# Attention with decay and a routed layer in one kernel: slot ids and gates in a table of their own, stores of x one step later, five last tiles through one-hot products

## The chip, the cores and the metric

The kernel runs on one core of a Trainium2 chip. The metric is the time of one execution on the device, in microseconds (us); the median of three runs is compared.

## The reference

There are 4 batches, 8 heads, 768 positions and a head dimension of 48, all in float32. First comes an attention whose state decays per channel, then a layer that sends each row to one of 8 experts:

```
for t in range(S):
    state = alpha[:, :, t, :, None] * state + einsum('bhd,bhe->bhde', k[:, :, t], v[:, :, t])
    y[:, :, t] = einsum('bhd,bhde->bhe', q[:, :, t], state)
x = y.transpose(0, 2, 1, 3).reshape(3072, 384)
out = x.copy()
do_compute = x @ w_skip > 0
logits = x[do_compute] @ w_gate                 # 8 experts
e_idx, gate_w = argmax(logits), softmax(logits)[argmax]
out[row] = x[row] + gate_w * (relu(x[row] @ w1[e]) @ w2[e])   # rows with do_compute, e = e_idx[row]
```

Each expert has w1 of 384 x 1024 and w2 of 1024 x 384.

## The kernel before, in words

The rows of x are cut into 24 tiles of 128 positions. The attention loop of `static_path` has a step i for each tile; four batches take turns, so that tile i belongs to batch i % 4. It is a software pipeline: in step i the loads of tile i+4 are issued, the decay products of tile i+3 are made (`decay`: on VectorE the scans `pfx`, L250, and `sfx`, L258, then on POOL two products into `qka`, L261 and L262), the scores of tile i+1 (`scores`, `causal`), the output of tile i (`inter`, `outer`, `carry`, `intra`), and the rows of tile i-1 (`rows`): TensorE turns the output into rows of x and gate logits (`ps_g`), VectorE reduces the logits (L355) and ScalarE copies x out (L360). All instructions stand in the order of the code; each engine runs its own in that order, and so do the queues that issue DMAs (SyncE's, called SP, and POOL's).

SP's queue carries the loads of `qka` (two DMAs a tile, into one of 5 buffers, L237) and of `vt` (L240, 5 buffers), a store of each tile's x to `out` (L362), pieces of expert weights (`raw`, L515), and once the clearing of the slot table (`clear`, L152).

Routing finds for each row its expert and its place in that expert's list. The list is the table `xs` in DRAM: 3072 slots for each expert, two words each, a row's id and its gate. `scatter` (L497, on POOL) writes one tile's 128 pairs to their slots with an indirect DMA. The id is made by an iota on POOL (L359) into column 384 of the tile of x, the gate is copied or written into column 385, and the scatter reads these two columns. The first 256 slots of each expert are worked on; `empty` marks unused ones.

The first expert starts before the last tiles are in its list. The rows of tiles 0 to LATE-1 that belong to expert 0 are fetched by their ids: `early_rows` reads expert 0's slots (`meta0`, L450, which waits for the scatters so far) and `fetch_rows` gathers the rows from `out` (L457, two gathers on POOL). The tiles from LATE on, three before the change, enter by a product: `late_split` splits x into a high and a low half (ScalarE L479, POOL L480), `route_slot` makes a one-hot row `hot` of each row's slot (L443), and `late_rows` multiplies (L466). Gathered and multiplied rows meet in the same PSUM tiles `x0t` (`early_turn`, L472, adds the gathered ones); the zero rows which `clear_late` writes to `out` in the place of late tiles keep the gather harmless. The remaining scatters follow at the end of the loop. In the expert stage `metas` (L555) reads all slots, `gather` fetches the rows of the next experts, `up` and `down` (L607, L623) are the two matmuls in three products of high and low halves, and `split_pieces` (L531, L535) splits the next expert's weights. `guard` reads alpha again (L571) and tests its range on ScalarE (L575).

Of the kernel before, what the change touches and what calls it, by code (L numbers as in the profile page):

```python
# [42 lines left out]
RW = 2 * D + E + 1  # L43
XW = DM + 2
BIG = 32768.0
# [4 lines left out]
WARM0, WARMB = 12, 2  # L50
LATE = NT - 3
DECAY_MIN = 1e-18
# [3 lines left out]
class Kernel:  # L56
# [40 lines left out]
    def constants(self):  # L97
# [36 lines left out]
        self.slot = const.tile([P, NT, 1], U32, name="slot")  # L134
        self.gate = const.tile([P, NT], F32, name="gate")

# [46 lines left out]
    def attention_pools(self, st):  # L183
        tc, nc = self.tc, self.nc
        self.vp = st.enter_context(tc.tile_pool(name="vp", bufs=5))
        self.sc = st.enter_context(tc.tile_pool(name="sc", bufs=2))
        self.xp = st.enter_context(tc.tile_pool(name="xp", bufs=9))
        self.sm = st.enter_context(tc.tile_pool(name="sm", bufs=2))
# [157 lines left out]
    def rows(self, i):  # L346

        nc, w = self.nc, self.work[i]
        if i < NT - 1:
            pg = self.ps_g.tile([P, NP, RW], F32, name="ps_g")  # L350
        else:
            pg = self.ps_v.tile([P, NP, RW], F32, name="ps_v")
        for p in range(NP):
            nc.tensor.matmul(pg[:, p, :], lhsT=w["xt"][:PD, p, :], rhs=self.xw[:PD, p, :], start=True, stop=True)  # L354
        nc.vector.tensor_reduce(out=self.logit[:, i, :], in_=pg[:, :, 2 * D:].rearrange("p a e -> p e a"),  # L355
                                op=ALU.add, axis=AX.X)
        x = self.xp.tile([P, XW], F32, name="x")
        row = self.row(i)
        nc.gpsimd.iota(x[:, DM:DM + 1].bitcast(I32), pattern=[[0, 1]], base=row, channel_multiplier=1)  # L359
        nc.scalar.copy(out=x[:, 0:DM].rearrange("p (a w) -> p a w", a=NP), in_=pg[:, :, 0:2 * D])  # L360
        w["x"] = x
        nc.sync.dma_start(out=self.out[row:row + P, :], in_=x[:, 0:DM])  # L362

# [30 lines left out]
    def route_one(self, i):  # L394
# [16 lines left out]
        yield nc.vector.tensor_scalar(out=s1, in0=s1, scalar1=1e-9, scalar2=None, op0=ALU.add)  # L411
        yield nc.vector.reciprocal(self.work[i]["x"][:, DM + 1:DM + 2], s1)

# [32 lines left out]
    def early_rows(self):  # L446
# [5 lines left out]
        self.early = [ins.ins.name]  # L452
        self.fetch_rows(self.xr0, meta)

# [20 lines left out]
    def late_split(self, i):  # L475

        nc, w = self.nc, self.work[i]
        hi, lo = w["parts"] = [self.late.tile([P, DM], F32R, name=f"late{n}{i}") for n in "hl"]
        nc.scalar.copy(out=hi, in_=w["x"][:, 0:DM])  # L479
        nc.gpsimd.tensor_tensor(lo, w["x"][:, 0:DM], hi.bitcast(F32), ALU.subtract)  # L480

# [10 lines left out]
    def scatter(self, i):  # L492
        nc = self.nc
        x = self.work[i]["x"]
        if i < SOLO:
            nc.gpsimd.tensor_copy(x[:, DM + 1:DM + 2], self.gate[:, i:i + 1])  # L496
        ins = nc.gpsimd.indirect_dma_start(  # L497
            out=self.xs[:, :], out_offset=bass.IndirectOffsetOnAxis(ap=self.slot[:, i, :], axis=0),
            in_=x[:, DM:DM + 2], in_offset=None, bounds_check=E * N - 1, oob_is_err=False)
        self.disjoint(ins.ins, "xs")  # L500
        if i >= LATE:
            for name in self.early:
                self.follow(ins.ins, name)
# [274 lines left out]
    def static_path(self, ctx):  # L778
# [8 lines left out]
        ends = {g[1] - 1: g for g in groups}  # L787
        pending, split, fetch = [], iter(()), iter(())

# [4 lines left out]
        with ExitStack() as st:  # L794
# [14 lines left out]
            for i in range(NT):  # L809
                if i + 4 < NT:  # L810
                    self.load(i + 4)
                if i == 2:
                    self.clear()
# [38 lines left out]
                self.outer(i)  # L852
                self.carry(i)
                if i == NT - 1:
                    assert not pending
                    self.early_rows()
                    self.intra(i)
                    self.route_rank(ends[i - 2])
                    self.small = self.route_slot(ends[i - 2])
                    self.tick(99)  # L860
                    ranked = ends[i - 2]
                if i == NT - 1:
                    self.rows(i - 1)
                if i < NT - 1:
                    self.intra(i)
                if ranked and SOLO - 1 <= i - 2 < LATE:
                    pending += range(*ranked)
                for _ in range(1 if i < SOLO else 2):
# [5 lines left out]
                if i - 1 in ends:  # L874
                    g = ends[i - 1]
                    self.small = chain(self.small, self.route_one(i - 1) if i - 1 >= SOLO else self.route_expert(g))
                    if i - 1 >= SOLO - 1:
                        self.tick(4 if i == NT - 1 else 99)
                    if i - 1 == LATE:
                        self.late_split(LATE)  # L880
            a, b = NT - 2, NT - 1
            self.late_split(a)
            self.rows(b)
            self.late_split(b)
            ps = self.ps_s.tile([P, 2, NP * P], F32, name="ps_s")
            self.x0t = [ps[:, 0, :CAP], ps[:, 1, :CAP], self.ps_g.tile([P, CAP], F32, name="ps_g")]
            self.route_rank((a, b))
            for k in range(KT):
                self.late_rows(LATE, k)
            self.early_turn(0)  # L890
# [12 lines left out]
            self.first_turn()  # L903
            for i in range(LATE, NT):
                self.scatter(i)
# [77 lines left out]
```

## Time and profile before

| what | before |
|---|---|
| median of three runs | 342.89 us (342.66 to 347.0) |
| the profiled execution | 343.51 us, of which 341.8 us are the span of its instructions |
| granted clock of TensorE, mean | 0.897 |
| busy: TensorE, VectorE, ScalarE, POOL | 298.9, 230.1, 153.3, 201.3 us |
| attention steps | to about 170 us |
| first matmul of the experts | 183.83 us |
| HBM read, written | 52.87 MB, 8.50 MB |

A row of the timeline has the start in us from the span's first instruction, the duration, the engine, the line of the kernel, the operation, the tiles (output <- inputs), and in brackets how long the engine was idle before it and what released it. SPq rows are DMAs being issued; they land later. PEld is the weight load of TensorE.

### The profile page before, as it was taken

To read this page: it belongs to the slowest core of one execution; us is meant where nothing else is said; L and a number is where in the kernel's file an instruction comes from. 1 tells how busy PE (TensorE), PEld (TensorE's weight loads), DVE (VectorE), ACT (ScalarE), POOL (GpSimd) and SP (SyncE) were. 2 spreads that over 40 slices of the span, in tenths; PEclk is the share of its full clock that TensorE was granted. 3 is DMA by queue.
4 is the path that set the end of the run, shared out by engine and by line. 5 is a ranking of instruction groups with operands and counts; after the bars stand their busy time and mean duration, and the time that the engine had idled before them with its cause. 6 is when DMAs were issued, how large, how long until landed. Compare 5 with 4: busy or idle time off the path is not lost. (4 is left out here: it accounts for less than half of the span.)

```text
span 341.8 us, 7389 instructions
## 1 busy us (share of the span) xinstructions
PE 298.9 (87%) x2778; PEld 276.1 (81%) x2778; DVE 230.1 (67%) x457; ACT 153.3 (45%) x300; POOL 201.3 (59%) x222
## 2 busy tenths in 40 slices
PE   6869869997997799889839699999989899999991
PEld 5758758886876688668729599999979899999990
DVE  8997495999999999998435623819265456555310
ACT  6114232533344344222531635959496885555200
POOL 6184254697787879757334575756647476764311
PEclk9658967996999969757978989999999999999998
DMA  8949898898669868942815174959769495741000
GB/s 231 294 90 146 186 213 221 207 189 200 177 140 188 207 130 173 191 135 74 125 40 146 37 232 153 381 172 318 263 223 338 148 360 202 244 160 66 16 22 23
DMA packets 27692, 60.33 MB, mean 177 GB/s; under 512 B 6944, under 2 KB 13646, under 8 KB 27648
## 3 DMA queue, kind: packets, MB, share of 16 engines
q1 hardware_dynamic: 24704, 54.67, 60.3%
q0 software_dynamic: 2944, 5.11, 4.4%
q8 instruction: 24, 0.39, 0.5%
q14 instruction: 20, 0.16, 0.2%
HBM read 52.87 MB, written 8.50 MB: 180 GB/s over the span
## 5 line engine op out<-in xcount | busy, mean ns | idle before, releaser
L261 POOL TENSOR_TENSOR qka<-qka,sfx 112x512 f32<-112x512 f32 x22 | 26.8, 1218 | 44.5 <-DVE sfx L258 30.0
L271 PE MATMUL ps_s<-qka 48*128 48x128 f32 x384 | 33.1, 320 | 19.8 <-POOL qka L261 12.1
L271 PEld LDWEIGHTS ps_s<-qka 48*128 48x128 f32 x384 | 28.3, 221 | 25.8 <-POOL qka L261 13.9
L612 DVE SCALAR_TENSOR_TENSOR hl<-ps_h,hh 128x512 fp32r<-128x512 f32 x32 | 22.0, 688 | 33.7 <-ACT hh L611 33.4
L623 PE MATMUL ps_o<-w2h,hh 128*128 128x384 f32 x128 | 44.2, 346 | 0.0
L623 PE MATMUL ps_o<-w2l,hh 128*128 128x384 f32 x128 | 43.6, 341 | 0.0
L623 PE MATMUL ps_o<-w2h,hl 128*128 128x384 f32 x128 | 43.5, 339 | 0.0
L497 POOL DMA_INDIRECT xs<-x,slot x24 | 31.1, 1298 | 10.4 <-POOL x L496 4.9
L535 POOL TENSOR_TENSOR w2l<-raw,w2h 128x512 fp32r<-128x512 f32 x24 | 31.3, 1304 | 9.4 <-ACT w2h L531 9.1
L607 PE MATMUL ps_h<-xh,w1h 128*128 128x256 f32 x192 | 34.2, 285 | 2.9 <-DVE hl L612 2.9
L258 DVE TENSOR_TENSOR_SCAN sfx<-qka,seedb 112x515 f32<-112x515 f32 x24 | 35.7, 1487 | 1.5
L360 ACT COPY x<-ps_g 128x384 f32<-128x384 f32 x23 | 11.0, 479 | 56.8 <-POOL qka L261 19.4
L628 POOL DMA_INDIRECT out_dram<-o,meta x16 | 18.3, 1146 | 30.3 <-DVE o L626 29.4
L535 POOL TENSOR_TENSOR w1l<-raw,w1h 128x512 fp32r<-128x512 f32 x16 | 22.0, 1377 | 23.7 <-issue 12.8
L250 DVE TENSOR_TENSOR_SCAN pfx<-qka,seed 112x516 f32<-112x516 f32 x24 | 31.8, 1327 | 6.0 <-DMA qka<-in_qka_dram 5.9
L327 ACT COPY xt<-ps_y 48x512 f32<-48x512 f32 x48 | 27.8, 580 | 14.1 <-PE ps_y L322 11.9
L607 PE MATMUL ps_h<-xh,w1l 128*128 128x256 f32 x192 | 33.7, 282 | 0.0
L322 PE MATMUL ps_y<-st,vt 128*48 128x128 f32 x384 | 33.4, 315 | 0.0
L607 PE MATMUL ps_h<-xl,w1h 128*128 128x256 f32 x192 | 33.1, 282 | 0.0
L626 DVE SCALAR_TENSOR_TENSOR o<-ps_o,meta,xr 128x384 f32<-128x384 f32 x16 | 9.9, 618 | 34.5 <-PE ps_o L623 34.3
L354 PE MATMUL ps_g<-xw,xt 112*128 112x105 f32 x184 | 31.2, 322 | 0.0
L278 DVE COPY_PREDICATED st<-mask,ps_s 128x1024 f32<-128x1024 uint8 x24 | 31.0, 1292 | 0.1
(144 smaller groups left out, 683.3 us busy)
## 6 DMA issues: line engine op xcount, KB each, us to landing
raw<-in_w_dram SPq DMA_DIRECT2D x64, 384.0 KB, 4.9
qka<-in_qka_dram SPq DMA_DIRECT2D x38, 288.9 KB, 5.2
vt<-in_v_dram SPq DMA_DIRECT2D x24, 192.0 KB, 5.1
out_dram<-x SPq DMA_DIRECT2D x24, 192.0 KB, 2.3
alpha<-in_nat_dram SPq DMA_DIRECT2D x8, 576.0 KB, 5.1
qka<-in_first_dram SPq DMA_DIRECT2D x3, 674.2 KB, 9.8
qka<-in_first_dram SPq DMA_DIRECT2D x2, 448.0 KB, 4.4
out_dram<-xr SPq DMA_DIRECT2D x3, 192.0 KB, 6.7
```

Source lines behind the costliest of these rows:

```text
L250: nc.vector.tensor_tensor_scan(pfx[:PD].rearrange("p a t -> p (a t)"), w["qka"][:PD, 0:n], self.seed1[:PD], 0.0, ALU.mult, ALU.max)
L258: nc.vector.tensor_tensor_scan(sfx[:PD, 0:n - 1][:, ::-1], w["qka"][:PD, 2:AW][:, ::-1], seed[:PD, 2:AW][:, ::-1], 0.0, ALU.mult, ALU.add)
L261: (eng or nc.gpsimd).tensor_tensor(w["kh"][:PD], w["kh"][:PD], after, ALU.mult)
L271: nc.tensor.matmul(ps[:, h, p * P:(p + 1) * P], lhsT=kh[r, p, :], rhs=qh[r, p, :], start=True, stop=True)
L278: self.nc.vector.copy_predicated(w["st"], self.mask, w["ps"])
L322: nc.tensor.matmul(ps[h][64 * h:64 * h + D, p, :], lhsT=v[:, o:o + D], rhs=w["st"][:, h, p * P:(p + 1) * P], start=(i < B and p == 0), sto ...
L327: nc.scalar.copy(out=xt[r], in_=ps[h][r])
L354: nc.tensor.matmul(pg[:, p, :], lhsT=w["xt"][:PD, p, :], rhs=self.xw[:PD, p, :], start=True, stop=True)
L497: ins = nc.gpsimd.indirect_dma_start(out=self.xs[:, :], out_offset=bass.IndirectOffsetOnAxis(ap=self.slot[:, i, :], axis=0), in_=x[:, DM:D ...
L535: eng.tensor_tensor(lo[:, s], raw[:, s], hi[:, s].bitcast(F32), ALU.subtract)
L607: nc.tensor.matmul(ps[:, u, :], lhsT=a[:, k, f * P:(f + 1) * P], rhs=b[:, k, :], start=(n == 0), stop=(n == len(order) - 1))
L623: nc.tensor.matmul(ps, lhsT=a[:, f, js], rhs=b[:, f, :], start=(n == 0), stop=(n == 3 * FT - 1))
```

## The change

Ids and gates move out of the tiles of x into one table `idg` of 128 x 24 x 2 words. A single iota at the start writes all ids; the routing writes the gates there, and `scatter` reads the table, without an iota or a copy of its own. The tiles of x lose two columns, and their pool goes from 9 buffers to 6.

The store of x leaves `rows` and becomes `store(i)`. It is issued at the head of a step, behind the loads of that step, for the tile whose rows were made one step earlier.

LATE goes from 21 to 19: five tiles enter through one-hot products instead of three. Accordingly the read of expert 0's slots is issued at the end of step 21 and the gathers at the end of step 22, two of the remaining scatters stand in steps 22 and 23, and two of the late products stand ahead of the last tile's `rows`.

```
-LATE = NT - 3
+LATE = NT - 5
...
+        self.idg = const.tile([P, NT, 2], F32, name="idg")
+        nc.gpsimd.iota(self.idg[:, :, 0:1].bitcast(I32).rearrange("p (c b) w -> p c b w", b=B),
+                       pattern=[[P, C], [S, B], [0, 1]], base=0, channel_multiplier=1)
+        self.gate = self.idg[:, :, 1]
...
-        self.xp = st.enter_context(tc.tile_pool(name="xp", bufs=9))
+        self.xp = st.enter_context(tc.tile_pool(name="xp", bufs=6))
...
-        x = self.xp.tile([P, XW], F32, name="x")
-        row = self.row(i)
-        nc.gpsimd.iota(x[:, DM:DM + 1].bitcast(I32), pattern=[[0, 1]], base=row, channel_multiplier=1)
-        nc.scalar.copy(out=x[:, 0:DM].rearrange("p (a w) -> p a w", a=NP), in_=pg[:, :, 0:2 * D])
-        w["x"] = x
-        nc.sync.dma_start(out=self.out[row:row + P, :], in_=x[:, 0:DM])
+        x = self.xp.tile([P, DM], F32, name="x")
+        nc.scalar.copy(out=x.rearrange("p (a w) -> p a w", a=NP), in_=pg[:, :, 0:2 * D])
+        w["x"] = x
+
+    def store(self, i):
+        row = self.row(i)
+        self.nc.sync.dma_start(out=self.out[row:row + P, :], in_=self.work[i]["x"])
...
     def scatter(self, i):
         nc = self.nc
-        x = self.work[i]["x"]
-        if i < SOLO:
-            nc.gpsimd.tensor_copy(x[:, DM + 1:DM + 2], self.gate[:, i:i + 1])
         ins = nc.gpsimd.indirect_dma_start(
             out=self.xs[:, :], out_offset=bass.IndirectOffsetOnAxis(ap=self.slot[:, i, :], axis=0),
-            in_=x[:, DM:DM + 2], in_offset=None, bounds_check=E * N - 1, oob_is_err=False)
+            in_=self.idg[:, i, :], in_offset=None, bounds_check=E * N - 1, oob_is_err=False)
...
                 if i + 4 < NT:
                     self.load(i + 4)
+                if i >= 2:
+                    self.store(i - 2)
...
-                if i == NT - 1:
-                    assert not pending
-                    self.early_rows()
-                    self.intra(i)
-                    self.route_rank(ends[i - 2])
+                self.intra(i)
+                if i == NT - 1:
+                    ranked = ends[i - 2]
+                    self.route_rank(ranked)
...
-                    if i - 1 == LATE:
-                        self.late_split(LATE)
+                if i - 1 >= LATE:
+                    self.late_split(i - 1)
+                if i == LATE + 2:
+                    assert not pending
+                    self.early_rows()
+                if i == LATE + 3:
+                    self.fetch_rows(self.xr0, self.meta0)
+                if i > LATE + 2 and after:
+                    self.scatter(after.pop(0))
             a, b = NT - 2, NT - 1
...
+            for k in range(KT - 1):
+                for i in range(LATE, a - 1):
+                    self.late_rows(i, k)
             self.rows(b)
+            self.store(a)
             self.late_split(b)
...
             self.route_rank((a, b))
+            for i in range(LATE, a - 1):
+                self.late_rows(i, KT - 1)
             for k in range(KT):
-                self.late_rows(LATE, k)
+                self.late_rows(a - 1, k)
             self.early_turn(0)
...
             self.first_turn()
-            for i in range(LATE, NT):
+            self.store(b)
+            for i in after + [a, b]:
                 self.scatter(i)
```

In SP's queue, this stood in steps 1 to 3 before; `qka1` takes tile 6, `qka2` tile 7, and `x_341` and `x_402` are the x of tiles 0 and 1:

```order
L240 DMA vt_307<-in_v_dram 128x384
L362 DMA out_0_dram<-x_341 128x384
L237 DMA qka1_133<-in_qka_dram 48x1541 x2
L240 DMA vt_367<-in_v_dram 128x384
L152 DMA xs_80<-empty_72 128x8x4
L362 DMA out_0_dram<-x_402 128x384
L237 DMA qka2_134<-in_qka_dram 48x1541 x2
```

The same stretch of SP's queue now (`x_342` is tile 0's):

```order
L243 DMA vt_308<-in_v_dram 128x384
L240 DMA qka1_133<-in_qka_dram 48x1541 x2
L243 DMA vt_366<-in_v_dram 128x384
L366 DMA out_0_dram<-x_342 128x384
L155 DMA xs_80<-empty_72 128x8x4
L240 DMA qka2_134<-in_qka_dram 48x1541 x2
```

Each store of x has moved behind the loads of the next tile; the clearing of `xs` keeps its place between the loads of tiles 6 and 7.

On POOL, the end of the attention loop before, from step 21 on; the number in `latel21` is the tile's, and `xr0` takes the gathered rows:

```order
L359 IOTA x_2018 128x1
L497 DMA xs_80<-x_1851,slot_200 24576x2
L497 DMA xs_80<-x_1944,slot_200 24576x2
L359 IOTA x_2091 128x1
L497 DMA xs_80<-x_2018,slot_200 24576x2
L480 TENSOR_TENSOR latel21_2126<-x_2091,lateh21_2125 128x384
L457 DMA xr0_107<-out_0_dram,meta0_2140 128x384 x2
L359 IOTA x_2174 128x1
L480 TENSOR_TENSOR latel22_2194<-x_2174,lateh22_2193 128x384
L359 IOTA x_2203 128x1
L480 TENSOR_TENSOR latel23_2208<-x_2203,lateh23_2207 128x384
L497 DMA xs_80<-x_2091,slot_200 24576x2
```

and now, from step 20 on, with the scatters of tiles 16 and 17 in the first row:

```order
L498 DMA xs_80<-idg_201,slot_200 24576x2 x2
L484 TENSOR_TENSOR latel19_1948<-x_1912,lateh19_1947 128x384
L498 DMA xs_80<-idg_201,slot_200 24576x2
L484 TENSOR_TENSOR latel20_2022<-x_1989,lateh20_2021 128x384
L484 TENSOR_TENSOR latel21_2096<-x_2066,lateh21_2095 128x384
L461 DMA xr0_107<-out_0_dram,meta0_2025 128x384 x2
L498 DMA xs_80<-idg_201,slot_200 24576x2
L484 TENSOR_TENSOR latel22_2164<-x_2146,lateh22_2163 128x384
L498 DMA xs_80<-idg_201,slot_200 24576x2
L484 TENSOR_TENSOR latel23_2189<-x_2185,lateh23_2188 128x384
L498 DMA xs_80<-idg_201,slot_200 24576x2 x3
```

The gathers of expert 0 stand behind the scatter of tile 18 instead of that of tile 20; behind them come five scatters instead of three, two of them among the low halves.

More of the change, by code (lines that the diff above doesn't have):

```diff
@@ L43 @@
 RW = 2 * D + E + 1
-XW = DM + 2
 BIG = 32768.0
@@ L134, in constants @@
         self.slot = const.tile([P, NT, 1], U32, name="slot")
-        self.gate = const.tile([P, NT], F32, name="gate")
+        self.idg = const.tile([P, NT, 2], F32, name="idg")
+        nc.gpsimd.iota(self.idg[:, :, 0:1].bitcast(I32).rearrange("p (c b) w -> p c b w", b=B),
+                       pattern=[[P, C], [S, B], [0, 1]], base=0, channel_multiplier=1)
+        self.gate = self.idg[:, :, 1]
     def first_slots(self):
@@ L411, in route_one @@
         yield nc.vector.tensor_scalar(out=s1, in0=s1, scalar1=1e-9, scalar2=None, op0=ALU.add)
-        yield nc.vector.reciprocal(self.work[i]["x"][:, DM + 1:DM + 2], s1)
+        yield nc.vector.reciprocal(self.gate[:, i:i + 1], s1)
     def route_rank(self, g):
@@ L452, in early_rows @@
         self.early = [ins.ins.name]
-        self.fetch_rows(self.xr0, meta)
+        self.meta0 = meta
     def fetch_rows(self, xr, meta):
@@ L478, in late_split @@
         hi, lo = w["parts"] = [self.late.tile([P, DM], F32R, name=f"late{n}{i}") for n in "hl"]
-        nc.scalar.copy(out=hi, in_=w["x"][:, 0:DM])
-        nc.gpsimd.tensor_tensor(lo, w["x"][:, 0:DM], hi.bitcast(F32), ALU.subtract)
+        nc.scalar.copy(out=hi, in_=w["x"])
+        nc.gpsimd.tensor_tensor(lo, w["x"], hi.bitcast(F32), ALU.subtract)
     def first_turn(self):
@@ L787, in static_path @@
         ends = {g[1] - 1: g for g in groups}
-        pending, split, fetch = [], iter(()), iter(())
+        pending, after, split, fetch = [], [], iter(()), iter(())
         def advance(it, n):
@@ L853, in static_path @@
                 self.carry(i)
+                self.intra(i)
                 if i == NT - 1:
-                    assert not pending
-                    self.early_rows()
-                    self.intra(i)
-                    self.route_rank(ends[i - 2])
-                    self.small = self.route_slot(ends[i - 2])
+                    ranked = ends[i - 2]
+                    self.route_rank(ranked)
+                    self.small = self.route_slot(ranked)
                     self.tick(99)
-                    ranked = ends[i - 2]
-                if i == NT - 1:
                     self.rows(i - 1)
[L864 to L867, printed above, removed]
+                if ranked and i - 2 >= SOLO - 1:
+                    (pending if i - 2 < LATE else after).extend(range(*ranked))
                 for _ in range(1 if i < SOLO else 2):
@@ L878, in static_path @@
                         self.tick(4 if i == NT - 1 else 99)
-                    if i - 1 == LATE:
-                        self.late_split(LATE)
-            a, b = NT - 2, NT - 1
-            self.late_split(a)
+                if i - 1 >= LATE:
[7 more added lines that the diff above has]
+                    self.scatter(after.pop(0))
+            a, b = NT - 2, NT - 1
+            ps = self.ps_s.tile([P, 2, NP * P], F32, name="ps_s")
+            self.x0t = [ps[:, 0, :CAP], ps[:, 1, :CAP], None]
+            for k in range(KT - 1):
+                for i in range(LATE, a - 1):
+                    self.late_rows(i, k)
             self.rows(b)
+            self.store(a)
             self.late_split(b)
-            ps = self.ps_s.tile([P, 2, NP * P], F32, name="ps_s")
-            self.x0t = [ps[:, 0, :CAP], ps[:, 1, :CAP], self.ps_g.tile([P, CAP], F32, name="ps_g")]
+            self.x0t[2] = self.ps_g.tile([P, CAP], F32, name="ps_g")
             self.route_rank((a, b))
+            for i in range(LATE, a - 1):
+                self.late_rows(i, KT - 1)
             for k in range(KT):
-                self.late_rows(LATE, k)
+                self.late_rows(a - 1, k)
             self.early_turn(0)
```

## The prediction

> **What bounds the kernel now.** I read the table of stretches first, to see which engine is full in which stage.
>
> ```profile
> 120.00:140.00 20.00, 18.62 (x231) 16.06 (x230) 19.75 (x37) 7.84 (x17) 16.57 (x20) 0.83 0.76 164
> 220.00:240.00 20.00, 19.74 (x138) 19.53 (x138) 10.95 (x17) 15.33 (x29) 12.53 (x10) 1.00 0.76 263
> ```
>
> The columns are the busy time of PE, PEld, DVE, ACT and POOL, then the granted clock, the DMA share and GB/s. From 120 to 140 us VectorE is busy 19.8 us of 20: the attention loop is VectorE's. From 200 us on the experts are TensorE's, 19.7 of 20. Time can be won only where neither holds: before 60 us, and in the hand-over from 160 to 198 us. Early on, the DMA queue of SyncE shows this:
>
> ```profile
> 17.79 0.35 SPq L240 DMA_DIRECT2D vt<-in_v_dram  x1
> 26.22 0.36 SPq L362 DMA_DIRECT2D out_dram<-x  x1
> 26.67 0.85 SPq L237 DMA_DIRECT2D qka<-in_qka_dram  x2
> 27.95 0.35 SPq L240 DMA_DIRECT2D vt<-in_v_dram  x1
> 28.35 0.42 SPq L152 DMA_DIRECT2D xs<-empty  x1
> 31.68 0.36 SPq L362 DMA_DIRECT2D out_dram<-x  x1
> 32.14 1.48 SPq L237 DMA_DIRECT2D qka<-in_qka_dram  x2
> ```
>
> Nothing is issued from 18.2 to 26.2 us: the store of x of tile 0 waits for ScalarE, and the load of tile 6 (26.67) stands behind it. The next store (31.68) holds up the load of tile 7 (32.14). The bandwidth from 0 to 60 us, in slices of 1.5 us, shows a silence of three slices (22.5 to 27) and, after the clearing of xs at 28.35 (1024 pieces of 16 bytes, by its shape), three slices at 48 to 81 GB/s (33 to 37.5):
>
> ```profile
> GB/s 0 201 296 290 291 319 292 324 290 274 302 298 170 147 10 0 0 0 271 226 128 152 65 48 81 167 180 363 335 199 251 232 229 154 172 199 213 242 191 283
> ```
>
> VectorE pays. Its first scan of tile 7 starts at 41.44, 9.3 us after the load was issued:
>
> ```profile
> 41.44 1.23 DVE L250 TENSOR_TENSOR_SCAN pfx<-qka,seed 112x516 f32<-112x516 f32 x1 [4.70 <-DMA qka<-in_qka_dram]
> ```
>
> TensorE then runs dry and gets half clock from 46 to 56 us (third number from the end of the next row). The waits from 15 to 60 us count 5.2 us of VectorE for two loads, so 0.5 beside the 4.7, for tile 6, and 2.5 for TensorE at half clock:
>
> ```profile
> 46.00:56.00 10.00, 9.90 (x85) 8.59 (x84) 7.74 (x20) 2.84 (x6) 4.69 (x8) 0.50 0.83 205
> ...
> DVE pfx L250 <- DMA qka<-in_qka_dram: 5.2, 2, 4.7
> DVE logit L355 <- PE ps_g L354: 2.5, 2, 1.3
> ```
>
> The second place is the hand-over. POOL from step 22 on:
>
> ```profile
> 166.48 0.99 POOL L497 DMA_INDIRECT xs<-x,slot  x1 [3.42 <-DVE on L403]
> ...
> 175.97 1.06 POOL L457 DMA_INDIRECT xr<-out_dram,meta  x1 [6.04 <-DMA meta<-xs]
> 177.33 1.00 POOL L457 DMA_INDIRECT xr<-out_dram,meta  x1 [0.31 <-issue]
> 178.35 0.14 POOL L359 IOTA x<- 128x1 int32 x1
> 178.45 1.00 POOL L480 TENSOR_TENSOR latel<-x,lateh 128x384 fp32r<-128x384 f32 x1
> ...
> 182.52 1.00 POOL L497 DMA_INDIRECT xs<-x,slot  x1 [0.81 <-DVE x L412]
> 183.82 0.97 POOL L497 DMA_INDIRECT xs<-x,slot  x1 [0.30 <-issue]
> ```
>
> and what hangs on it on TensorE: the gathered rows of expert 0, the last one-hot products, the first matmul of the experts, and the first transposes of expert 1.
>
> ```profile
> 179.04 1.22 PE L472 MATMUL ps_s<-ident,xr 128*128 128x128 f32 x4 [5.38 <-DMA xr<-out_dram,meta]
> ...
> 183.44 0.28 PE L466 MATMUL ps_g<-hot,lateh 128*128 128x256 f32 x1
> 183.56 0.28 PE L466 MATMUL ps_g<-hot,latel 128*128 128x256 f32 x1
> 183.83 0.38 PE L607 MATMUL ps_h<-xh,w1h 128*128 128x256 f32 x1
> ...
> 195.98 0.77 PE L587 MATMUL ps_x<-ident,xr 128*128 128x128 f32 x3 [3.26 <-DMA xr<-out_dram,meta]
> ```
>
> The chain is: scatter of tile 20 (166.48), 9.49 us, over its landing and the read of expert 0's slots, to the gather (175.97), 7.85 us of POOL work to the last scatter (183.82), and 12.16 us, over the read of all slots and the gather of expert 1, to the transposes (195.98), for which TensorE waits 3.26 us. Everything behind moves with it.
>
> **The change, term by term.** The base is the profiled execution, 343.51 us, which is 0.62 above the median of the runs (342.89).
>
> *Early loads.* With the store behind the loads, the load of tile 6 goes out at about 18.2 (right behind the vt of tile 5), into the silence, so the 0.5 us go. The vt of tile 6 still waits for a buffer until 27.95, as before. Then come the store of tile 0 (0.45), the clearing (0.42) and the load of tile 7 at about 29.2 instead of 32.14. If it lands 9.3 us after its issue again, the scan starts at 38.5. If the slow slices belong to the clearing, which keeps its place, the load gains only what no longer stands ahead of it, and in the worst case lands at 41.4 as now. VectorE is ready at 36.2 (41.44 less 5.2). Bounds: 0 and 5.2 us. I take a scan at 39.5, between the two: **-1.9 us**. TensorE's idle time shrinks by as much, with VectorE's wait down to 3.3 us; I count nothing for the clock, since the stretch from 120 to 140 us (first row above) has a clock of 0.83, though TensorE idled only 1.38 us in all of it. The Trainium skill ("TensorE: Matmul & The Clock Gate", Part 1) has the clock halve after a whole idle window of about 3.4 us. By that rule the shortened gap would keep full clock and most of the 2.5 us would go too; the row from 120 to 140 us speaks against it.
>
> *Middle, 60 to 150 us.* POOL loses 24 iotas (0.14 us in the rows above) and 18 copies. VectorE is the full engine there, so this is worth nothing directly. What moves is when POOL and VectorE collide: each scatter starts some 0.5 us sooner. VectorE can lose much to a POOL operation. Here its scan, 1.23 us at 41.44, takes 2.92 beside the low half of a weight:
>
> ```profile
> 143.00 2.92 DVE L250 TENSOR_TENSOR_SCAN pfx<-qka,seed 112x516 f32<-112x516 f32 x1
> 143.54 1.28 POOL L535 TENSOR_TENSOR w2l<-raw,w2h 128x512 fp32r<-128x512 f32 x1
> ```
>
> But a scan that starts 0.06 us behind a scatter loses nothing:
>
> ```profile
> 69.09 1.02 POOL L497 DMA_INDIRECT xs<-x,slot  x1 [0.28 <-POOL x L496]
> 69.15 1.23 DVE L258 TENSOR_TENSOR_SCAN sfx<-qka,seedb 112x515 f32<-112x515 f32 x1
> ```
>
> One or two such 1.7 us collisions may come or go, bounds -3 and +3; I take **-0.3**. Two more clearing stores at step 14 cost SyncE some 0.9 us (0.45 each, as the stores above), hidden in a step of 5.5 us (the loads at 26.67 and 32.14 are a step apart).
>
> *Hand-over.* POOL's scatter of tile 18 is now the last one before the read of expert 0's slots. POOL's queue ahead of it starts where the last decay product ends, at 157.33:
>
> ```profile
> 156.16 1.17 POOL L262 TENSOR_TENSOR qka<-qka,pfx 112x512 f32<-112x512 f32 x1
> ...
> 159.16 0.19 ACT L407 ACTIVATION_READ_ACCUMULATOR ex<-d 128x1 f32 x1
> ...
> 168.35 0.49 ACT L479 CAST lateh<-x 128x384 fp32r<-128x384 f32 x1
> ```
>
> Two scatters of 1.0 us with gaps of 0.3 bring it to 159.9. The low half of tile 19 needs its high half, a ScalarE cast of 0.49 us (as at 168.35) behind the row at 159.16, so it runs from 159.9 to 160.9. The scatter starts at 161.2, 5.3 us before that of tile 20 now. With the same 9.49 us, the gathers start at 170.7 instead of 175.97. From there POOL's chain is longer: two more scatters, 2 x 1.3 us, stand between the gathers and the end, against two iotas less and half of the 0.81 us wait, so 9.8 us instead of 7.85. The last scatter starts at 180.5, **-3.3 us**. TensorE gets its last low half at 177.7, does nine matmuls at 0.12 us apart and starts the experts at 178.9, 4.9 us sooner. That is more than can be kept: the transposes of expert 1 still follow the last scatter, at 192.7, and TensorE waits 4.7 us for them instead of 3.26. The 12 added matmuls (1.4 us) lie in the 5.4 us that TensorE now waits for the gather (row at 179.04); the two added casts, low halves and one-hot rows lie in steps 20 to 22, behind the last decay work (156.16). If that cover were gone the additions would cost TensorE 1.4 us and POOL 2.0. Bounds of the term: -4.9 (if the transposes did not wait) and +2.0 (if the gathers started no earlier and POOL's chain only grew).
>
> Sum: -1.9 - 0.3 - 3.3 = -5.5, so 338.0 against the profiled 343.51; by the median, 0.6 lower, **337.4 us**.
>
> **Rivals.**
>
> *The early wait goes wholly.* Tile 7 lands in time, 5.2 us saved, TensorE keeps its clock and the 2.5 us behind it go: 343.5 - 7.7 - 0.3 - 3.3 = 332.2, by the median 331.6. For it: the silence until 27 is used. Against it: the clearing and tile 7's load still meet. Chance 0.25. The clock rule of the Trainium skill cited above would make this case the likeliest once the gap is under its window; no row here bears that out.
>
> *The hand-over gives nothing.* The stages change but the read of expert 0's slots waits as long (tile 18's scatter is held on POOL by the low halves), and POOL's two added scatters eat what is left. The early term alone remains: 341.6, by the median 341.0. Chance 0.18. That the loads don't move at all (the vt load ahead of the store waits as long as the store did) belongs here too; then 343.
>
> *Scatters now collide with the scans*, slower. Without iota and copy ahead of it, a scatter can start ahead of VectorE's scan instead of inside it, and hold it up as the low half at 143.54 did. If each of the 16 scatters of steps 6 to 19 cost VectorE 0.8 of its 1.0 us, that is 12.8 us: 343.5 + 12.8 - 5.2 = 351.1, by the median 350.5. It decides from 0.33 us a scatter, where it eats all of the gain. The row at 69.15 speaks against it. Chance 0.07. The Trainium skill ("SBUF — State Buffer", section "SBUF: two separate sides") says that whichever of VectorE and GpSimd starts first gets the shared pair of ports for the whole instruction. By that rule the scatter that comes first would cost the scan up to 1.0 us; the scan at 69.15 took 1.23 us, its undisturbed time, so this trace does not bear it out for scatters.
>
> **How the numbers follow.** The forecast (335.5 to 340.5) has 0.50, the rivals 0.25, 0.18 and 0.07. The range, 331 to 343.5, takes in the full early gain and the case of no gain at the hand-over, and leaves out the collisions. About 2% of 342.9, 6.9 us, is what a measurement of this kernel can tell from no change: faster means below 336.0. Faster gets the first rival and the low end of the forecast, 0.25 + 0.12 = 0.37; slower, above 349.7, 0.05 of the 0.07; the rest, 0.58, is within.
>
> **What the new profile would show.** The load of tile 6 issued near 18 us and that of tile 7 near 29; the scan of tile 7 with a wait of about 3 us; the read of expert 0's slots near 5 us earlier relative to the last decay product; the last scatter some 23 us behind that product instead of 26.5; TensorE's wait ahead of the transposes of expert 1 grown to 4 or 5 us. I am wrong if VectorE's scans grow longer on average, if tile 7 lands as late as now, or if the experts take longer once they have begun.

## The result, and the profile after

The changed kernel takes 332.85 us (median of 4 runs, 329.62 to 333.8) beside 343.01 us for the kernel before: a ratio of 0.9661, with a 95% interval of 0.9565 to 0.9758. Measured again with 6 runs it gave 334.72 us beside 341.78, a ratio of 0.9736 (0.966 to 0.9812). Ratios are formed from undisturbed executions only. So it is 2.6 to 3.4% faster, though the interval of the second measurement reaches to a difference of 1.9%. The forecast was 337.4 us, too high by 2.7 to 4.6 us; the range, 331.0 to 343.5, holds both medians. The case that got the most weight, a difference within 2%, did not come.

The profiled execution took 333.16 us, with a span of 331.4 (341.8 before). Five starts cut the span into stretches that can be compared between kernels: the first scans of tiles 7, 10 and 23 on VectorE, the last scatter on POOL, and the last result of the experts. In the timeline of the changed kernel they are:

```profile
37.34 1.23 DVE L253 TENSOR_TENSOR_SCAN pfx<-qka,seed 112x516 f32<-112x516 f32 x1 [1.49 <-DMA qka<-in_qka_dram]
54.94 1.29 DVE L253 TENSOR_TENSOR_SCAN pfx<-qka,seed 112x516 f32<-112x516 f32 x1
142.93 1.23 DVE L253 TENSOR_TENSOR_SCAN pfx<-qka,seed 112x516 f32<-112x516 f32 x1
170.69 0.97 POOL L498 DMA_INDIRECT xs<-idg,slot  x1 [0.30 <-issue]
323.77 0.62 DVE L627 SCALAR_TENSOR_TENSOR o<-ps_o,meta,xr 128x384 f32<-128x384 f32 x1 [3.61 <-PE ps_o L624]
```

and in that of the kernel before, where tile 7 and the last scatter have been shown:

```profile
60.84 1.23 DVE L250 TENSOR_TENSOR_SCAN pfx<-qka,seed 112x516 f32<-112x516 f32 x1
152.17 1.23 DVE L250 TENSOR_TENSOR_SCAN pfx<-qka,seed 112x516 f32<-112x516 f32 x1
334.28 0.62 DVE L626 SCALAR_TENSOR_TENSOR o<-ps_o,meta,xr 128x384 f32<-128x384 f32 x1 [3.61 <-PE ps_o L623]
```

The differences of such starts, in us, for the traces that the argument needs (each is one execution; "changed, again" is a second one of the same kernel, whose run took 335.5 us; "store", "table" and "hand-over" are the kernel before with one part of the change):

| stretch | before | changed | changed, again | store | table | hand-over | changed, POOL's short work back |
|---|---|---|---|---|---|---|---|
| to tile 7 | 41.44 | 37.34 | 40.31 | 36.57 | 42.12 | 41.26 | 37.73 |
| tile 7 to 10 | 19.40 | 17.60 | 17.86 | 17.74 | 19.68 | 19.19 | 18.49 |
| tile 10 to 23 | 91.33 | 87.99 | 88.01 | 91.01 | 86.51 | 90.79 | 91.31 |
| tile 23 to last scatter | 31.65 | 27.76 | 27.82 | 31.03 | 30.72 | 28.86 | 30.99 |
| last scatter to last result | 150.46 | 153.08 | 152.18 | 150.40 | 151.39 | 149.53 | 149.68 |

The last result comes 10.5 us sooner (the whole span is 10.4 us shorter): -4.1, -1.8, -3.3, -3.9 and +2.6 us, in this order.

The queue of SyncE in the changed kernel answers to the one shown of before:

```profile
19.06 0.35 SPq L243 DMA_DIRECT2D vt<-in_v_dram  x1
19.50 0.84 SPq L240 DMA_DIRECT2D qka<-in_qka_dram  x2
25.96 0.35 SPq L243 DMA_DIRECT2D vt<-in_v_dram  x1
26.40 0.38 SPq L366 DMA_DIRECT2D out_dram<-x  x1
26.83 0.43 SPq L155 DMA_DIRECT2D xs<-empty  x1
27.36 1.35 SPq L240 DMA_DIRECT2D qka<-in_qka_dram  x2
```

Tile 6's load goes out at 19.50 instead of 26.67 and tile 7's at 27.36 instead of 32.14. The load of tile 7 still takes 10 us to its scan, and VectorE still waits 1.49 us for it. TensorE keeps full clock in this trace where it had 0.50 before:

```profile
46.00:56.00 10.00, 9.13 (x142) 7.83 (x143) 9.83 (x16) 3.60 (x7) 5.66 (x5) 1.00 1.04 272
```

At the hand-over, POOL's timeline in the changed kernel is:

```profile
146.94 1.17 POOL L265 TENSOR_TENSOR qka<-qka,pfx 112x512 f32<-112x512 f32 x1
...
151.77 0.99 POOL L498 DMA_INDIRECT xs<-idg,slot  x1 [0.17 <-issue]
155.38 0.99 POOL L484 TENSOR_TENSOR latel<-x,lateh 128x384 fp32r<-128x384 f32 x1 [2.63 <-ACT lateh L483]
159.87 1.00 POOL L484 TENSOR_TENSOR latel<-x,lateh 128x384 fp32r<-128x384 f32 x1 [3.49 <-ACT lateh L483]
161.01 1.05 POOL L461 DMA_INDIRECT xr<-out_dram,meta  x1 [0.15 <-issue]
```

From the last decay product's end (148.11) to the last scatter (170.69) it is now 22.6 us, 26.5 before. The gather starts 9.24 us behind the scatter of tile 18 but waits for no DMA: it stands behind the low half of tile 21 in POOL's own queue. TensorE then pays at the rows of expert 1, twice, and at half clock:

```profile
182.46 0.70 PE L588 MATMUL ps_x<-ident,xr 128*128 128x128 f32 x3 [3.48 <-DMA xr<-out_dram,meta]
184.30 0.90 PE L588 MATMUL ps_x<-ident,xr 128*128 128x128 f32 x3 [1.14 <-DMA xr<-out_dram,meta]
```

```profile
182.00:190.00 8.00, 6.40 (x23) 6.02 (x24) 1.11 (x2) 3.03 (x6) 6.79 (x7) 0.57 0.57 174
```

The half clock lasts from 182.7 to 189.5 us, against 196.2 to 199.6 before: twice as long. This is where part of the lead of 13.1 us at the last scatter goes. TensorE's waits from the first matmul of the experts to the last result (total us, number, longest) are, before and in the changed kernel:

```profile
PE ps_x L587 <- DMA xr<-out_dram,meta: 3.7, 2, 3.3
PE ps_h L607 <- DVE hl L612: 2.9, 3, 1.6
...
PE ps_x L588 <- DMA xr<-out_dram,meta: 4.6, 2, 3.5
PE ps_h L608 <- DVE hl L613: 3.6, 2, 2.1
```

### The profile page after: what moved, and what is told of

It is laid out like the page before. It is cut to its first block, busy times and chain, and to the rows that moved or that the text cites. A ratio compares the mean times of both kernels' runs of the same rounds, so it can differ in the third digit from the quotient of the medians.

```text
span 331.4 us, 7353 instructions
## 1 busy us (share of the span) xinstructions
PE 289.4 (87%) x2790; PEld 267.5 (81%) x2790; DVE 228.6 (69%) x459; ACT 154.3 (47%) x302; POOL 192.1 (58%) x183
## 4 chain that ended last, share of the span: by engine, by line
PE 38%; DVE 28%; DMA 15%; issue 7%; ACT 7%; SPq 2%; POOL 1%; POOLq 0%; DVEq 0%; ACTq 0%
PE ps_o L624 13%; PE ps_h L608 13%; DVE pfx L253 6%; DMA qka<-in_qka_dram 6%; DVE sfx L261 6%; DVE st L281 6%; DMA alpha<-in_nat_dram 5%; DMA raw<-in_w_dram 3%; ACT over L576 3%; PE ps_y L303 3%; PE ps_g L357 2%; PE ps_y L325 2%; DVE w1l L536 1%; ACT w2h L532 1%; PE ps_s L274 1%
## 5 line engine op out<-in xcount | busy, mean ns | idle before, releaser
L274 PE MATMUL ps_s<-qka 48*128 48x128 f32 x384 | 30.4, 300 | 17.4 <-POOL qka L264 10.5
L274 PEld LDWEIGHTS ps_s<-qka 48*128 48x128 f32 x384 | 25.8, 202 | 23.2 <-POOL qka L264 11.7
L624 PE MATMUL ps_o<-w2l,hh 128*128 128x384 f32 x128 | 44.3, 346 | 0.0
L612 ACT ACTIVATE hh<-ps_h 128x512 fp32r<-128x512 f32 x32 | 19.1, 596 | 28.9 <-PE ps_h L608 24.6
L261 DVE TENSOR_TENSOR_SCAN sfx<-qka,seedb 112x515 f32<-112x515 f32 x24 | 31.2, 1300 | 1.8 <-DVE eq L384 0.4
L325 PE MATMUL ps_y<-st,vt 128*48 128x128 f32 x384 | 30.9, 299 | 1.1 <-issue 1.1
L608 PEld LDWEIGHTS ps_h<-xh,w1h 128*128 128x128 f32 x192 | 28.0, 189 | 4.6 <-DVE hl L613 4.4
```

The source lines that it names most:

```text
L261: nc.vector.tensor_tensor_scan(sfx[:PD, 0:n - 1][:, ::-1], w["qka"][:PD, 2:AW][:, ::-1], seed[:PD, 2:AW][:, ::-1], 0.0, ALU.mult, ALU.add)
L274: nc.tensor.matmul(ps[:, h, p * P:(p + 1) * P], lhsT=kh[r, p, :], rhs=qh[r, p, :], start=True, stop=True)
L325: nc.tensor.matmul(ps[h][64 * h:64 * h + D, p, :], lhsT=v[:, o:o + D], rhs=w["st"][:, h, p * P:(p + 1) * P], start=(i < B and p == 0), sto ...
L608: nc.tensor.matmul(ps[:, u, :], lhsT=a[:, k, f * P:(f + 1) * P], rhs=b[:, k, :], start=(n == 0), stop=(n == len(order) - 1))
L612: nc.scalar.activation(out=hh, in_=ps, func=AF.Relu)
L624: nc.tensor.matmul(ps, lhsT=a[:, f, js], rhs=b[:, f, :], start=(n == 0), stop=(n == 3 * FT - 1))
```

## The experiments

**One part of the change at a time.** First the store alone:

```diff
 (in rows)
-        nc.sync.dma_start(out=self.out[row:row + P, :], in_=x[:, 0:DM])
 (at the head of step i, behind the loads)
+                if i >= 2:
+                    self.store(i - 2)
```

> The kernel before with the later store alone: iota, copy and LATE as before. Theory A (the order in SP's queue explains all of the 9.2 us that the attention loop gained: tile 7 lands earlier, TensorE then keeps its clock from 46 to 56 us, and from there the scans meet fewer of POOL's operations): tile 7's first scan near 37.3, no half clock from 46 to 56 us, last decay product 9 us earlier, time near 343.0 - 9.2 = 333.8. Theory B (the queue gives only the early part; the 3.3 us between tile 10 and tile 23 come from POOL's shorter queue, without iotas and copies): 343.0 - 5.9 = 337.1. The prediction's own terms: 1.9 us early, so 341.1, with the half clock still there.

It took 337.38 us beside 342.1, a ratio of 0.9852 (0.9807 to 0.9897). The scan of tile 7 starts at 36.57 us with a wait of 0.69, and the stretch from 46 to 56 us has full clock:

```profile
36.57 1.32 DVE L250 TENSOR_TENSOR_SCAN pfx<-qka,seed 112x516 f32<-112x516 f32 x1 [0.69 <-DMA qka<-in_qka_dram]
```

So the whole of the early gain, 6.5 us to tile 10, belongs to the queue's order. But from tile 10 to 23 it takes 91.01 us, against 91.33 before. Theory A falls, theory B stands so far.

Then the table alone:

```diff
-        self.gate = const.tile([P, NT], F32, name="gate")
+        self.idg = const.tile([P, NT, 2], F32, name="idg")   # one iota writes all ids; gate = column 1
 (in rows)
-        nc.gpsimd.iota(x[:, DM:DM + 1].bitcast(I32), ...)
 (in scatter)
-            nc.gpsimd.tensor_copy(x[:, DM + 1:DM + 2], self.gate[:, i:i + 1])
-            in_=x[:, DM:DM + 2], ...
+            in_=self.idg[:, i, :], ...
```

> The kernel before with the table of ids and gates alone: no iota a tile, no copy ahead of a scatter; stores and LATE as before. Theory A: within 1 us of 343.0, tile 7's scan still at 41.4. Theory B: about 3.3 us of the middle come from here, 339.7, with fewer scans of 2.9 us. The prediction's term: -0.3, 342.7.

The runs went from 335.97 to 342.76 us, with a median of 340.53 beside 342.1, and give no ratio; the trace decides here. Tile 7 is as late as before (42.12), and from tile 10 to 23 it takes 86.51 us, 4.8 less than before. This is what theory B says.

And the hand-over alone (the lines of the change that belong to LATE, with iota, copy and store as before):

```diff
-LATE = NT - 3
+LATE = NT - 5
```

> The kernel before with five one-hot tiles in place of three alone, and the order of the hand-over that goes with it; iota, copy and stores as before. The attention loop is as before (last decay product at 157.3). Theory C (the hand-over gains 3.9 us and gives back 2.7 in the expert stage, since TensorE waits longer for the rows of expert 1 and then gets two stretches of half clock instead of one): 343.0 - 1.2 = 341.8, with two half-clock stretches behind the transposes of expert 1. Rival D (what is given back comes from elsewhere, so that the hand-over alone keeps its gain): 343.0 - 3.9 = 339.1, one stretch. The prediction's term: -3.3, 339.7.

It took 339.06 us beside 342.1, a ratio of 0.984 (0.9721 to 0.9959). From tile 23 to the last scatter it gained 2.8 us and nothing was given back behind it (149.53 us). TensorE waited 2.63 and 0.70 us for the rows of expert 1, and one stretch of half clock followed (192.1 to 195.5). So rival D is nearer than theory C: in this trace five one-hot tiles cost the experts nothing.

**POOL's short work put back.** This asks whether the 3.3 us of the middle are the iotas and copies themselves:

```diff
+        self.spare = const.tile([P, NT, 2], F32, name="spare")
 (in rows)
+        nc.gpsimd.iota(self.spare[:, i, 0:1].bitcast(I32), pattern=[[0, 1]], base=self.row(i), channel_multiplier=1)
 (in scatter)
+        if i < SOLO:
+            nc.gpsimd.tensor_copy(self.spare[:, i, 1:2], self.gate[:, i:i + 1])
```

> The changed kernel with 24 iotas and 18 one-column copies put back on POOL at their old places, but writing to a spare table that nothing reads; the scatter still reads the table of ids and gates. Theory B (the 3.3 us and more that the table saves between tiles 10 and 23 are these short instructions: each delays POOL's scatter and low half into VectorE's scans): 88.0 us between the first scans of tiles 10 and 23 become about 91, time 332.9 + 3 = 335.9. Rival L (it is the table itself, whose scatters wait for nothing of the tile of x): 88.0 us stay, 332.9.

It took 337.36 us beside 344.86 (0.9819, 0.9721 to 0.9916). The stretch from tile 10 to 23 is back at 91.31 us, against 87.9 to 88.8 in every trace with the changed kernel's POOL. The first scans of tiles 10 and 23 with the short work back are:

```profile
56.22 1.23 DVE L254 TENSOR_TENSOR_SCAN pfx<-qka,seed 112x516 f32<-112x516 f32 x1 [0.71 <-DMA qka<-in_qka_dram]
147.53 1.23 DVE L254 TENSOR_TENSOR_SCAN pfx<-qka,seed 112x516 f32<-112x516 f32 x1
```

That the short instructions cost these 3.3 us is shown, and rival L falls. Tile 12 shows one way in which it happens. With the short work, POOL's queue and VectorE's scans (timeline of this kernel) are:

```profile
68.46 0.15 POOL L363 IOTA spare<- 128x1 int32 x1
68.55 0.31 POOL L501 COPY spare<-idg 128x1 f32<-128x1 f32 x1
69.01 1.83 POOL L502 DMA_INDIRECT xs<-idg,slot  x1 [0.15 <-issue]
70.86 1.28 POOL L540 TENSOR_TENSOR w1l<-raw,w1h 128x512 fp32r<-128x512 f32 x1
...
68.76 1.23 DVE L254 TENSOR_TENSOR_SCAN pfx<-qka,seed 112x516 f32<-112x516 f32 x1
70.31 2.92 DVE L262 TENSOR_TENSOR_SCAN sfx<-qka,seedb 112x515 f32<-112x515 f32 x1
```

and in the changed kernel:

```profile
67.15 1.03 POOL L498 DMA_INDIRECT xs<-idg,slot  x1
68.21 1.28 POOL L536 TENSOR_TENSOR w1l<-raw,w1h 128x512 fp32r<-128x512 f32 x1
...
67.21 1.22 DVE L253 TENSOR_TENSOR_SCAN pfx<-qka,seed 112x516 f32<-112x516 f32 x1
68.75 1.84 DVE L261 TENSOR_TENSOR_SCAN sfx<-qka,seedb 112x515 f32<-112x515 f32 x1
```

Without iota and copy the scatter starts 0.06 us ahead of the first scan, and neither loses. With them it starts 0.25 us inside the scan, lasts until 0.85 us behind the scan's end, and pushes the low half of a weight into the middle of the second scan, which takes 2.92 us instead of 1.84. The Trainium skill ("SBUF — State Buffer", section "SBUF: two separate sides") says that while a VectorE operation in a two-port mode runs, GpSimd is locked out of the shared ports and cannot write the descriptors of a DMA that it issues. That a scan is such an operation is not shown here, but the scatter inside the scan took 1.83 us instead of 1.03, which goes the same way. The grouped rows of POOL between tiles 10 and 23 show what its queue loses in all, of before:

```profile
L497 POOL DMA_INDIRECT xs<-x,slot x16 | 23.2, 1448 | 4.7 <-POOL x L496 4.4 <-DVE tmp L339 0.3
L496 POOL COPY x<-gate 128x1 f32<-128x1 f32 x15 | 7.3, 487 | 0.0
L359 POOL IOTA x<- 128x1 int32 x13 | 1.7, 130 | 0.0
```

and of the changed kernel:

```profile
L498 POOL DMA_INDIRECT xs<-idg,slot x16 | 20.2, 1260 | 3.5 <-issue 2.6 <-DMA out_dram<-x 0.5 <-DVE eq L409 0.3
```

Copies of one column cost 7.3 us here, 0.49 each, and the 16 scatters took 3.0 us more. On VectorE the 26 scans of tiles 10 to 22 add up to 38.7 us before, 35.3 with the short work back and 32.6 in the changed kernel. So with the short work back 2.7 of the 3.3 us could be longer scans; how much of that reached the time, and where the rest comes from, is not shown. VectorE as a whole was busy for less time there than in the changed kernel (81.6 us against 83.5) and idled more.

With the short work back the hand-over lost as well (30.99 us against 27.76), and the traces show another cause there. The rows are the stretch from tile 23 to the last scatter, before, with the short work back, and changed:

```profile
152.17:183.82 31.65, 25.10 (x244) 21.50 (x240) 16.32 (x79) 10.13 (x27) 15.97 (x23) 0.79 0.45 97
147.53:178.52 30.99, 28.66 (x261) 24.78 (x258) 19.21 (x82) 11.31 (x30) 17.63 (x24) 0.77 0.38 102
142.93:170.69 27.76, 25.30 (x261) 21.70 (x258) 18.67 (x82) 11.20 (x30) 16.50 (x17) 0.90 0.40 112
```

With the short work back TensorE is at half clock until 161.8 us, 14.2 us into this stretch; in the changed kernel it is so until 148.6, 5.7 us into it. A group of 16 products `ps_y` then takes 1.95 us instead of 1.08, ScalarE copies it later, and the high halves for which POOL waits (4.93 and 3.72 us) stand behind these copies. In every trace of the table that took over 30 us here the clock was 0.72 to 0.79, in the others 0.88 to 0.90. Why the half clock lasted longer was not tested.

**The clearing one step earlier.**

```diff
-                if i == 2:
+                if i == 1:
                     self.clear()
```

> The changed kernel with the clearing of xs issued one step earlier, behind the loads of tile 5 instead of behind the store of tile 0. Theory E (the 1024 small pieces of the clearing slow the load of tile 7, which follows them): tile 7 lands in time, its scan loses its wait of 1.5 us, time near 332.9 - 2 = 330.9. Rival F (the load of tile 7 is late because it is issued late, behind the vt of tile 6 that waits for its buffer): it is issued 0.4 us earlier and gains no more, or the pieces now slow tile 6: 332.5 to 334.

It took 329.73 us beside 342.1 (0.9636, 0.9551 to 0.9721); this interval overlaps that of the changed kernel, so the trace has to say what came of it. The load of tile 7 is issued at 26.89 and lands in time. Its scan starts at 35.76 without a wait, though the load goes out only 0.47 us sooner:

```profile
35.76 2.09 DVE L253 TENSOR_TENSOR_SCAN pfx<-qka,seed 112x516 f32<-112x516 f32 x1
```

Theory E: the load's issue had been moved by the change, but its landing belonged to the clearing ahead of it. The same holds in the three later experiments that also clear earlier: the scan of tile 7 waits for no load, although in one of them the load goes out only at 29.16; in the second trace of the changed kernel it waits 3.3 us for a load issued at 30.41. By tile 10 the lead over the changed kernel is down to 0.8 us (54.17 against 54.94). The other 2.6 us of this trace's lead arose in the expert stage (150.52 us to the last result), where the waits for the rows of expert 1 were 2.8 and 0.9 us and one stretch of half clock followed. That part comes and goes between executions.

**What the wait for expert 1 costs.** Zero matmuls fill it:

```diff
 (in turn, ahead of the transposes)
+            if e == 1:
+                for _ in range((8, 2)[j]):
+                    nc.tensor.matmul(ps[:, 0, :], lhsT=zero, rhs=zero, start=True, stop=True)
```

> The changed kernel with 8 and 2 matmuls of zeros ahead of the two sets of transposes of expert 1, into PSUM that the transposes overwrite: about 3.3 and 0.8 us at the 0.41 us a piece of the zero matmuls at the start, inside the waits of 3.48 and 1.14 us. Theory G (the wait takes TensorE's clock, and the half clock from 182.7 to 189.5 us is what the expert stage gives back): no half clock there, the first result of expert 0 3 us earlier behind the last scatter, time 332.9 - 3 = 329.9. Rival H (the half clock comes without the wait, or what was given back belongs to a late gather): within 1 us of 332.9.

It took 332.9 us beside 344.86 (0.968, 0.9582 to 0.9779), no better than the changed kernel. Locally theory G holds: the clock stays full,

```profile
184.00:194.00 10.00, 8.64 (x56) 8.26 (x55) 3.52 (x6) 3.83 (x8) 8.40 (x8) 1.00 0.61 187
```

and the first result of expert 0 comes 17.22 us behind the last scatter instead of 20.78. The Trainium skill ("TensorE: Matmul & The Clock Gate", Part 1) ties half clock to an idle window of about 3.4 us. This pair of traces agrees (3.48 us of waiting with half clock behind it, 1.06 without), but half clock also came behind shorter waits: 2.63 us with the hand-over alone, and 1.73 and 1.04 us close together with the store alone. From there to the last result it takes 133.34 us instead of 132.30, so 2.5 of the 3.6 us are kept in the trace. But the early loads were late in this execution (tile 7 at 39.15), and the median does not show the gain.

**The wait filled with work.** The transposes of expert 1 move behind the first half of expert 0's second product:

```diff
-                if e + 1 < E:
+                if 0 < e < E - 1:
                     self.turn(e + 1)
 ...
                     self.down(e, j)
+                    if (e, j) == (0, 0):
+                        self.turn(1)
```

> The changed kernel with the transposes of expert 1 behind the first half of expert 0's second product instead of ahead of it. The prediction held that the hand-over's gain is cut by TensorE's wait for these rows. Theory J (the wait is the bound: 24 matmuls of 0.175 us, 4.2 us, now lie in it): the waits of 3.48 and 1.14 us go, and with them half clock of some 3 us; time 332.9 - 4.6 - 3 = 325. Rival K (the wait only moves: the first matmuls of expert 1 wait for its transposed rows, or the first results wait for the rows of expert 0, which are gathered last): 331 to 333.

It took 334.18 us beside 344.86 (0.9705, 0.9595 to 0.9814). The wait for the rows is gone (0.7 us left), and the first result comes 14.95 us behind the last scatter, 5.8 less than in the changed kernel. Yet all of it is lost before the second expert's first result; the waits of TensorE in this kernel's expert stage name it:

```profile
PE ps_h L608 <- DVE hl L613: 7.5, 3, 5.0
PE ps_x L588 <- DMA xr<-out_dram,meta: 0.7, 1, 0.7
```

VectorE's `hl` waits for ScalarE's relu `hh`, and ScalarE's timeline shows what stands ahead of that relu:

```profile
198.10 1.25 ACT L576 ACTIVATE over<-alpha,lim 128x1152 bf16<-128x1152 f32 x1 [9.11 <-DMA alpha<-in_nat_dram]
...
200.74 0.58 ACT L612 ACTIVATE hh<-ps_h 128x512 fp32r<-128x512 f32 x1
```

It is the range test of alpha, queued 9 us ahead of its data. Rival K, in a form that it had not named. With the clearing moved as well it was the same:

> The changed kernel with the clearing one step earlier and the transposes of expert 1 behind the first half of expert 0's second product. If the two are independent: 329.7 less what the transposes' place gives: 322 to 324 by theory J, 328 to 330 by rival K.

333.33 us beside 344.86 (0.9708, 0.9599 to 0.9816), with 7.3 us of TensorE's waiting for `hl`.

**The test of alpha moved.** In the changed kernel ScalarE stands before every other piece of alpha within about 1 us of the issue of its load. Now the loads are spread, and go out 4.7 to 13.4 us before their tests start:

```diff
 (in the loop over g, behind up)
+                    if e and g == 1:
+                        advance(check, 1)
 (in the loop over j, behind down)
-                    advance(check, 1)
+                    if j == 0:
+                        advance(check, 1)
```

> The changed kernel with the range test of alpha moved: each of its eight pieces is loaded and tested about ten microseconds apart (in the middle of an expert's first product and behind the first half of its second) instead of a load behind each half, so that ScalarE reaches a test some ten microseconds after the load was issued, not four. Theory M (what the expert stage gives back goes to ScalarE, which stands 7.7, 4.5, 3.6 and 5.0 us before a test of alpha while the relu of the next expert is queued behind it): these waits shrink below 1 us each, TensorE's 3.6 us of waiting for VectorE's low half of h go, time 332.9 - 3.5 = 329.4. Rival N (the weights of the next experts are late anyway, behind the same loads): the wait of TensorE turns into one for weights, 332 to 333.

> The changed kernel with the clearing one step earlier, the transposes of expert 1 behind the first half of expert 0's second product, and the test of alpha moved as in the run before. Theory M: the 7.3 us for which TensorE waited for VectorE when only the first two were done go, and the lead at the second result of expert 0 (18.4 us behind the last scatter instead of 25.0) is kept to the end: 332.9 - 6.6 - 1 = 325.3. Rival N: TensorE waits for weights in their place, 330 to 333.

> The changed kernel with the clearing one step earlier and the test of alpha moved, the transposes of expert 1 at their place of the changed kernel. Theory M: 329.7 - 3 = 326.7 with the waits for the rows of expert 1 (3.5 and 0.9 us) still there; rival N: 329 to 331.

> The changed kernel as it is, beside the three before it on the same chip, to compare medians: 0.966 of the kernel before, as measured, so that differences of 1% between it and the three can be told.

All four ran on one chip, beside 341.78 us for the kernel before:

| kernel | median, us | ratio to before | last scatter to last result, us |
|---|---|---|---|
| changed | 334.72 | 0.9736 (0.966 to 0.9812) | 152.18 |
| changed, test of alpha moved | 330.32 | 0.963 (0.9557 to 0.9702) | 148.41 |
| the same, clearing earlier | 327.82 | 0.9568 (0.95 to 0.9636) | 147.00 |
| the same, transposes moved | 322.47 | 0.9409 (0.9342 to 0.9477) | 142.07 |

Theory M holds. With the test moved TensorE no longer waits for `hl`, and now the transposes' place is worth 5.35 us, where without that it was worth nothing. In the last kernel the largest wait for alpha is 1.5 us, and TensorE is busy without a gap from 200 to 300 us:

```profile
ACT over L576 <- DMA alpha<-in_nat_dram: 2.5, 4, 1.5
```

```profile
200.00:300.00 100.00, 100.00 (x707) 99.83 (x706) 56.91 (x92) 70.50 (x130) 62.21 (x50) 1.00 0.71 242
```

In the kernel before, the same two rows are

```profile
ACT over L575 <- DMA alpha<-in_nat_dram: 21.3, 4, 7.9
```

```profile
200.00:300.00 100.00, 97.13 (x680) 96.34 (x679) 51.43 (x83) 67.33 (x124) 62.13 (x50) 1.00 0.73 256
```

This version beats both kernels.

## Why the prediction was right or wrong

*Early loads (-1.9).* The step was right: the loads went out earlier, at 19.5 (18.2 forecast) and 27.4 (29.2), and the clearing kept tile 7 late, as the earlier clearing showed. The size varies from execution to execution, and the queue shows one reason: the load of `vt` of tile 6, which stands ahead of the load of tile 7 and waits for a buffer, was forecast at 27.95 and went out at 25.96 in one trace of the changed kernel and at 29.00 in the other. The scan of tile 7 was forecast at 39.5; in the two traces of the changed kernel it starts at 37.34 and 40.31, so the gain was 4.1 and 1.1 us. In the second one the scans of tiles 3 and 4 were already late.

*Nothing for the clock.* Here the forecast fell short. From tile 7 to tile 10 another 1.8 and 1.5 us were gained in the two traces. In the first trace the clock stayed full, as the cited rule had it and the row from 120 to 140 us did not. But the clock is not the account: in the second trace it was at half from 45.9 to 52.8, and this stretch still took 17.86 us. What shortened it was not tested.

*Middle (-0.3).* **This term was mis-sized**, and it is the step that failed. It measured -3.3 us in both traces, a little outside its bounds of 3, and -4.8 with the table alone; put back, the short instructions undo it to 0.02 us. The argument was that POOL's short work costs nothing directly because VectorE is the full engine, and that one or two collisions of 1.7 us may come or go. But a part of VectorE's busy time was waiting for POOL inside its scans (38.7 us for 26 scans before, 32.6 after), so VectorE's busy time was not its work. Nor was it the bound by itself: with the changed kernel's POOL VectorE was busy 80.9 to 85.4 us in traces whose stretch was 87.9 to 88.8 us in all. The third rival looked at the right place with the wrong sign: in tile 12 a scatter that starts ahead of the scan is the good case, and one that starts inside it is the costly one.

*Hand-over (-3.3).* The size was near: -3.9 and -3.8. POOL's chain from the gather to the last scatter, forecast at 9.8 us, measured 9.68; the last scatter stands 22.6 us behind the last decay product, 23 forecast. The gathers start 12.9 us behind that product (13.4 forecast), but it was POOL's low half that held them and not the read of the slots, so that this agreement is in part luck. The hand-over alone gave -2.8; the table and the store alone gave -0.9 and -0.6 in the same stretch. And the new order does not secure the gain: with POOL's short work back, and TensorE at half clock for longer, it gave only -0.7. The clock, for which the prediction counted nothing, may decide here; how much of the -3.9 us is the order's own is not shown.

*What the experts make of it.* The first wait of TensorE for expert 1 was forecast to grow from 3.26 to 4.7 us (by the forecast's own times it would be 4.9). It measured 3.48, and the second one grew from 0.44 to 1.14. What was missed is what follows it: 2.6 and 1.7 us more to the last result than before, which the prediction had named as a sign that it would be wrong. From the first matmul of the experts, which now starts 0.6 us ahead of the last scatter, it is 3.2 us more (153.69 us against 150.45). The traces divide this: TensorE is busy 1.5 us longer (145.31 against 143.84), with 6.8 us of half clock instead of 3.4, waits 0.9 us more for the rows of expert 1 and 0.7 us more for `hl`. The waits for `hl` hang on ScalarE's tests of alpha: with the transposes moved the first result was 5.8 us sooner, and the time was the same until the tests were moved too. This division is read from one trace each; with POOL's short work back 6.8 us of half clock went with 149.68 us from the last scatter, less than before.

The first rival (331.6 us) was nearest to the first median, and the forecast to the second; the rival's reason held only in part, since its early gain of 7.7 us measured 5.9 and 2.7 to tile 10. That both medians lie inside the range is partly luck: in the first trace the attention loop to tile 23 gave 9.2 us where 2.2 were forecast, and the experts took 2.6 back.

## What to carry to other kernels

An engine that is busy all the time may be waiting inside its instructions: compare the same instruction's duration along the trace before a neighbour's short work is called free. When work is moved out of a wait and the time stays, look for the next engine that stands in its queue ahead of data, and move that as well; here one move was worth nothing until the second was made, and the two with the earlier clearing took 12 us off the changed kernel. Look at the granted clock of a stretch before its gain is credited to a new order. Profile the changed kernel twice before a term of 2 or 3 us is called measured, since the first loads alone differed by that much.

## What the runs showed of the hardware

- A scatter on POOL that began 0.06 us ahead of a VectorE scan took 1.03 us and the scan 1.22; one that began 0.25 us inside a scan took 1.83 us, and the scan behind it 2.92.
- A copy of one column (128 x 1) on POOL cost 0.49 us on average in the attention loop, about as much as a cast of 128 x 384 on ScalarE.
- The clearing of 1024 pieces of 16 bytes ahead of a load delayed its landing: with the issue at 27.36 and 26.89 us, the scan waited 1.49 us in the one case and not at all in the other, where the clearing had gone out 7.5 us before.
- 8 zero matmuls of 128 x 128 in the wait took 1.95 us, 0.24 each; a gap of 1.06 us was left, and the clock stayed at 1.00. Waits of 3.48 us (changed) and of 2.63 us (hand-over alone) were followed by half clock.
